# Splitting doubles on a Trainium2 core: the masked exponent and its product kept in the contiguous temporary

## The chip, the cores and the metric

One core of one Trainium2 chip runs the kernel. The metric is the device time of one execution in microseconds; before the change it is 879.73 us, the median of three runs (878.51 to 879.98). The engines are TensorE (PE, with PEld for its weight loads), VectorE (DVE), ScalarE (ACT), GpSimd (POOL) and SyncE (SP, which issues the DMAs).

## The reference

Attention with pooled queries feeds a two-layer feed-forward network, and that feeds a second network of four experts mixed by probabilities:

```python
q_pool = q.reshape(B, H, S // 2, 2, D).mean(axis=3)          # 2 x 8 heads, 1152 -> 576 queries, D = 64
scores = scale * np.matmul(q_pool, k.transpose(0, 1, 3, 2))
attn = softmax(scores); x = np.matmul(attn, v)               # -> 1152 tokens x 512
h = x @ w_in;  x = np.maximum(0.01 * h, h) @ w_out           # 512 -> 2048 -> 512
p = probs / (probs.sum(-1, keepdims=True) + 1e-09)
out = sum(p[:, e:e + 1] * (np.maximum(x @ w1[e], 0.0) @ w2[e]) for e in range(4))   # 512 -> 1024 -> 512
```

`w_in` and `w_out` reach the kernel as doubles (the set-up multiplies them by a float64 number), so each of these weights is a pair of 32-bit words in memory; the experts' weights are float32.

## The kernel before, in words

Every operand of a product is split into a higher part `h` that TensorE's float32r holds and a lower part `l`, the rest; a product is three matmuls (h by h, h by l, l by h). For the doubles this is the work of `split64` (from line 59): a tile of 128 x 512 doubles lies in SBUF as interleaved words, `L` the lower and `W` the upper word of each pair, so that both are read and written with a step of two words. `split64` returns six steps:

- s0: ACT writes the scaled upper word into a temporary `t` (L69). It is contiguous, and there are two of them in turn (tag `c` in the feed-forward stage, `kh` while the attention still runs).
- s1, s2: DVE shifts `t` (L72) and puts the sign back from `W` (L76). Without `fast`, ACT turns the lower word into a float in place (L78).
- s3: DVE masks sign and exponent of `t` into `W` (L83, called the mask below); ACT rounds `t` into `h` (L84); POOL writes `l = t - h` (L86, the subtraction).
- s4: the lower word times the masked power of two, into `L` (the product): on DVE with `fast` of 1 (L90), else on POOL (L92).
- s5: POOL adds the product to `l` (L95, the addition). With `fast` of 2, used for one weight tile only, DVE does the subtraction and the addition too.

The order of every engine's instructions is written out by hand (`manual_schedule`): each engine works through its own list, and an instruction that waits for another engine holds up all that stand behind it on its own engine. The first network's 16 tiles f of `w_in` (called a0 to a15) and of `w_out` (b0 to b15) are split as they are needed. What one f does after its first-layer matmuls is called a round here: `run(evac_leaky(f, ps), next_a(f + 2), next_b(f - 1))` interleaves the steps of the evacuation (ACT L600 and DVE L601 make `gf` out of PSUM, ACT L48 makes `gh`, DVE L55 makes `gl`) with those of two splits. `gf` has one buffer and PSUM's three-bank tiles `h` take turns between two, so a late L601 holds up TensorE's next first layer. The second layer runs in groups of tiles, one output quarter d behind each first layer: first a group of two tiles (18 matmuls a quarter, rounds 3 to 6), then groups of four, four and six (36 or 54 matmuls). L637 and L639 take those sums out of PSUM, ACT in the first group and DVE in the others. In round 15 the splits of b14 and of b15 stand one after the other ahead of the evacuation.

a0 and a1 are split during the last pair of the attention, one step for each tile of queries; a1's steps s4 and s5 stand behind the attention's last sums (`run_av(1e9)`, then `ahead` of 9 and 10). The pool of the feed-forward stage's temporaries `c` is opened in the space which the attention's pools leave, so its first tile waits for the last accesses there.

Of the kernel before, what the change touches and what calls it, by code (L numbers as in the profile page):

```python
# [13 lines left out]
U32 = mybir.dt.uint32  # L14
# [16 lines left out]
def f32(ap):  # L31
    return ap.bitcast(F32)
# [3 lines left out]
def tile_kernel(ctx: ExitStack, tc: tile.TileContext, q, k, v, w_in, w_out, probs, w1, w2, out):  # L36
# [22 lines left out]
    def split64(h, l, w, tmp, fast=0):  # L59
        """Parts of doubles, given as pairs of words: h of float32r, l with what h leaves. A list of steps, of which  # L60
        VectorE does one more with fast of 1 and all of GpSimd's with 2."""
        L, W = w[:, :, 0], w[:, :, 1]
        c = {}
        e = DVE if fast == 2 else POOL

        def s0():
            # The exponent with float32's bias: the word, read as float32, has it less 896 when scaled by 2**-112.
            c["t"] = tmp()
            ACT.mul(f32(c["t"]), f32(W), 2.0**-112)  # L69

        def s1():
            DVE.tensor_scalar(c["t"], c["t"], 3, None, op0=ALU.logical_shift_left)  # L72

        def s2():
            t = c["t"]
            DVE.scalar_tensor_tensor(t, W, -2**31, t, op0=ALU.bitwise_and, op1=ALU.bitwise_or)  # L76
            if not fast:
                ACT.mul(f32(L), L.bitcast(U32), 2.0**-52)  # L78

        def s3():  # L80
            # The lower 32 bits of the fraction, times the signed power of two.
            t = c["t"]
            DVE.tensor_scalar(W, t, -0x800000, None, op0=ALU.bitwise_and)  # L83
            ACT.copy(h, f32(t))  # L84
            # t has 21 bits and h their upper 12: l holds the difference exactly.
            e.tensor_tensor(l, f32(t), f32(h), op=ALU.subtract)  # L86

        def s4():
            if fast:
                DVE.scalar_tensor_tensor(f32(L), L.bitcast(U32), 2.0**-52, f32(W), op0=ALU.mult, op1=ALU.mult)  # L90
            else:
                POOL.tensor_tensor(f32(L), f32(L), f32(W), op=ALU.mult)  # L92

        def s5():
            e.tensor_tensor(l, f32(l), f32(L), op=ALU.add)  # L95

        return [s0, s1, s2, s3, s4, s5]

    def run(*lists):
        """The lists' steps in turn."""  # L100
        for i in range(max(map(len, lists), default=0)):
            for x in lists:
                if i < len(x) and x[i]:
                    x[i]()

# [1 line left out]
    n1 = DFF // 128  # L107
# [21 lines left out]
    def shared(i):  # L129
        """Two operands of 512 columns, where the attention has a tile of weights."""  # L130
        t = se.tile([128, S], F32R, tag=f"e{i}", name="sh", bufs=1)
        return t[:, :DM], t[:, DM:2 * DM]
# [52 lines left out]

    # Three banks of PSUM: the attention's scores; then in turn with three more.
    ps_h = [ctx.enter_context(tc.tile_pool(name="ps_h0", bufs=1, space=PSUM))]
    turn = [0]
# [18 lines left out]

    # ================= attention =================
    with ExitStack() as actx:
# [7 lines left out]
        for t in qst:  # L217
            POOL.memset(f32(t[:, :, 0, SQ:]), 0.0)
            POOL.memset(f32(t[:, :, 1, :64]), 0.0)
        # The lower parts of a pair's middle rows, each head's over its own partitions.  # L220
        qmid = [sb.tile([128, 128], F32R, tag=f"qmid{i}", name=f"qmid{i}", bufs=1) for i in range(2)]
# [6 lines left out]
        def two_heads(n, name):  # L228
            """Operands of a pair, of which every other's stay after the attention, for weights as they are loaded."""
            pool = sb if n % 2 else se  # L230
            return [pool.tile([128, S], F32R, tag=f"{name}{h}", name=name, bufs=1) for h in range(2)]
# [23 lines left out]
        def first_pair():  # L255
            """The first pair's operands; each head's rows come twice from memory, so nothing is moved between partitions."""
            b, p = pairs[0]
# [31 lines left out]
        def prep_pair(n):  # L289
            """The pair's operands, split, and the loads of the next; a list of steps."""  # L290
            # VectorE does what the first scores and products wait for.
            e_q, e_v = DVE if n == 1 else POOL, DVE if n == 0 else POOL
# [44 lines left out]

        # The q tiles of a pair: four of one head, one of 64 rows of each, four of the other.
        tiles = [(n, t) for n in range(len(pairs)) for t in range(9)]
        # The second product's share of a tile's time, in microseconds of TensorE, by the tile's place in its pair.  # L340
        AVD, AVB = 1.07, {1: 0.5}
        # How many tiles before a pair's first its operands are begun, and the tiles for the first pairs.
        P0, P1, P2 = 10, 1, 8
        # Up to this tile the scores run two tiles ahead, then three.
        L2 = 6
        # The last pair's tiles at which a feed-forward weight's split begins.
        AT0 = (0, 6)
        # Parts of the first layer that fit between the last four tiles.
        F0N = (0, 2, 2, 2)
        s_sb, chunks = {}, {}  # L350

        def emit_s(i):
            n, t = tiles[i]
            ps = three_banks(0)
            Q, K = qst[n % 2], kst[n]
            if t < 4:
                use = [(0, t * 128)]
            elif t == 4:
                use = [(0, 512), (1, 0)]
            else:  # L360
                use = [(1, 128 + (t - 5) * 128)]
            for c in range(3):
                cs = slice(c * CW, (c + 1) * CW)
                mms = [(Q[:, j, h, c0:c0 + 128], K[h][:, cs]) for h, c0 in use for j in (1, 0)]
                if len(use) > 1 and n:
                    # The rows' lower parts together, times the higher parts of both heads' keys.
                    mms = mms[::2] + [(qmid[n % 2], k_hi_of[n][:, cs])]
                for m, (x, y) in enumerate(mms):
                    PE.matmul(ps[:, c, :CW], x, y, start=m == 0, stop=m == len(mms) - 1)  # L369
            e = (sb if i % 5 > 2 else se).tile([128, S], F32, tag=f"e{i % 5}", name="e", bufs=1)  # L370
            e = e.rearrange("p (a b) -> p a b", a=3)
            st = sb.tile([128, 4], F32, tag="st", name="st", bufs=6)
            DVE.tensor_scalar(e, ps[:, :, :CW], -0.5 / float(D) ** 0.5, None,  # L373
                              op0=ALU.mult, op1=ALU.min, accum_out=st[:, 0:1])
            s_sb[i] = (e, st)
# [91 lines left out]
        with tc.manual_schedule():  # L467
            # The table of activation functions comes while the first loads run.
            DVE.memset(warm, 0.0)
            ACT.activation(warm, warm, AF.Exp)  # L470
            q_add, q_hi, q_lo, k_hi, k_lo = first_pair()
            # TensorE's clock rises while the first loads run.
            wps = ps_t.tile([128, 3, 128], F32, tag="t", name="t")
# [30 lines left out]

            # The feed-forward layers' first weights are split along with the last pair.

# [20 lines left out]

            # The operands of each pair are made ready from so many tiles before its first, the loads of the next in between.
            begin_at = {9 * m - P0: m for m in range(3, len(pairs))} | {0: 0, P1: 1, P2: 2}
            steps = {}  # L530
            for i, (n, t) in enumerate(tiles):
# [8 lines left out]
                if i == len(tiles) - 4:  # L540
                    # The last scores are done: the first layer starts with the tokens and heads that are ready.
                    f0_ps, mms = first_layer(0, xh, xl)
# [19 lines left out]

    # ================= feed-forward layers =================
    wb = ctx.enter_context(tc.tile_pool(name="wb", bufs=1))
# [13 lines left out]
    def next_b(f):  # L578
        """The f tile's second-layer weights; in the last layers those of two, at the second."""
        if f < n1:  # L580
# [10 lines left out]
    def evac_leaky(f, ps):  # L591
        """A list of steps, among which those of two calls of split64 fit."""
        s = ps[:, :, :CW]
# [80 lines left out]
    with tc.manual_schedule():  # L674
# [8 lines left out]
        run(evac_leaky(1, ps), next_b(1))  # L683
        # A second-layer tile takes the place of that eight before it, which is free when its group is done.
        when_b = {f: [f - 1] for f in range(3, 15)} | {15: [14, 15]}
        # A group's second layer runs among the next tiles' first layer.
        second = [(g, d) for g in range(len(GROUPS)) for d in range(KD)]
# [70 lines left out]
```

## Time and profile before

| | |
|---|---|
| time, median of three runs | 879.73 us (878.51 to 879.98) |
| span of the profiled execution, first to last instruction | 876.6 us |
| PE busy | 848.8 us, 97% |
| DVE, ACT, POOL busy | 472.5, 379.4, 382.6 us |
| chain that ended last | PE 75%, DVE 17%, issue 3%, ACT 2% |

The time of the profiled execution is its span of 876.6 us and what lies around it, the start and the end of the program; the page gives the span alone. A busy share is an average over stages: DVE's 40 slices read 9 in the attention and to about 350 us, then fall to 1 and 2 in the experts, so what DVE does matters in one part and not in another. In the views below a row of the timeline gives start and duration in us, the engine, the line, the operation with what it writes and reads, and in brackets the idle time before it with what ended that.

### The profile page before, as it was taken

The page shows a single profiled execution, that of the slowest core. Times are in us where ns is not written, and L with a number is a line of the kernel's source. Part 1 is how long each engine was busy: PE and PEld are TensorE (multiplying, and loading weights), DVE is VectorE, ACT ScalarE, POOL GpSimd, SP SyncE. Part 2 cuts the span into 40 slices and gives each one's busy share as a digit, 9 for nine tenths or more (in the row PEclk, how much of TensorE's full clock was granted, in tenths as well). Part 3 has the DMA queues.
Part 4 walks back from the last instruction along what each step waited for, and adds up shares of the span by engine and source line. Part 5 has one row for each costly group of instructions (what it writes and reads, how often), then busy time and mean ns, then how long its engine had stood idle before and what let it go on. Part 6 is the DMA issues. An engine that isn't in the chain of part 4 may idle for free.

```text
span 876.6 us, 12608 instructions
## 1 busy us (share of the span) xinstructions
PE 848.8 (97%) x4879; PEld 797.3 (91%) x4879; DVE 472.5 (54%) x814; ACT 379.4 (43%) x672; POOL 382.6 (44%) x330
## 2 busy tenths in 40 slices
PE   6799999999989899999999999999999999999998
PEld 5699999999989899999999998899988998889986
DVE  5989999999998999787733121112211111111211
ACT  4888998999874665334311330013200331013200
POOL 1678888898655677665510431013300332003200
PEclk7999999999999999999999999999999999999999
DMA  6446644664500233222310211001200121002011
GB/s 188 120 114 174 152 108 134 177 150 108 161 26 28 100 126 109 79 67 97 97 49 1 76 69 49 1 29 68 96 1 1 49 97 49 1 0 73 13 49 48
DMA packets 20795, 68.59 MB, mean 78 GB/s; under 512 B 2688, under 2 KB 2688, under 8 KB 20736
## 3 DMA queue, kind: packets, MB, share of 16 engines
q1 hardware_dynamic: 20736, 67.79, 26.1%
q8 instruction: 38, 0.62, 0.3%
q14 instruction: 21, 0.17, 0.1%
HBM read 48.91 MB, written 2.36 MB: 58 GB/s over the span
## 4 chain that ended last, share of the span: by engine, by line
PE 75%; DVE 17%; issue 3%; ACT 2%; POOL 1%; DMA 1%; SPq 0%; DVEq 0%; POOLq 0%; ACTq 0%
PE h L203 9%; PE h L205 9%; PE h L204 9%; PE o L664 8%; PE o L665 8%; PE o L666 8%; PE h L369 6%; PE av L438 5%; PE t L411 5%; DVE e L373 4%; DVE tl L55 3%; PE h L633 3%; PE h L632 3%; PE h L634 3%; DVE w L83 2%
## 5 line engine op out<-in xcount | busy, mean ns | idle before, releaser
L615 ACT ACTIVATE gh<-h 128x1152 fp32r<-128x1152 f32 x32 | 36.3, 1135 | 281.7 <-PE h L205 281.7
L616 DVE SCALAR_TENSOR_TENSOR gl<-h,gh 128x1152 fp32r<-128x1152 f32 x32 | 43.4, 1358 | 159.4 <-ACT gh L615 159.4
L55 POOL TENSOR_TENSOR a<-w,a 128x512 fp32r<-128x512 f32 x21 | 27.6, 1314 | 208.8 <-ACT a L48 208.8
L55 DVE TENSOR_TENSOR tl<-t,th 128x384 fp32r<-128x384 f32 (+1 forms) x240 | 112.0, 503 | 1.7 <-ACT th L415 1.6
L389 POOL TENSOR_SCALAR e<-e,st 128x1152 f32<-128x1152 f32 x70 | 86.9, 1244 | 57.4 <-DVE st L387 37.0
L369 PE MATMUL h<-k,qst 128*128 128x384 f32 x438 | 96.7, 352 | 12.6 <-DVE e L373 6.2
L373 DVE TENSOR_SCALAR_CACHE_REDUCE e<-h 128x1152 f32<-128x1152 f32 x72 | 97.4, 1353 | 16.6 <-PE h L369 15.8
L415 ACT CAST th<-t 128x384 fp32r<-128x384 f32 (+1 forms) x240 | 91.2, 458 | 24.9 <-PE t L411 24.7
L369 PEld LDWEIGHTS h<-k,qst 128*128 128x128 f32 x438 | 77.0, 195 | 17.8 <-DVE e L373 10.8
L379 ACT ACTIVATE e<-e,st 128x1152 f32<-128x1152 f32 x72 | 91.1, 1266 | 4.4 <-DVE e L373 2.0
L411 PE MATMUL t<-ident,e 128*128 128x128 f32 x648 | 84.4, 276 | 4.2 <-POOL e L389 2.6
L670 DVE SCALAR_TENSOR_TENSOR oacc<-o,pw,oacc 128x512 f32<-128x512 f32 x27 | 20.3, 751 | 125.0 <-PE o L666 125.0
L665 PE MATMUL o<-b,gh 128*128 128x512 f32 x216 | 85.2, 395 | 0.0
L664 PE MATMUL o<-b,gh 128*128 128x512 f32 x216 | 85.2, 394 | 0.0
L666 PE MATMUL o<-b,gl 128*128 128x512 f32 x216 | 85.2, 394 | 0.0
L203 PE MATMUL h<-yh,a 128*128 128x384 f32 x252 | 84.7, 336 | 0.0
L205 PE MATMUL h<-yh,a 128*128 128x384 f32 x252 | 84.7, 336 | 0.0
L204 PE MATMUL h<-yl,a 128*128 128x384 f32 x252 | 84.7, 336 | 0.0
L411 PEld LDWEIGHTS t<-ident,e 128*128 128x128 f32 x648 | 75.0, 141 | 10.1 <-POOL e L389 5.4
L55 POOL TENSOR_TENSOR sh<-w,sh 128x512 fp32r<-128x512 f32 x19 | 25.1, 1332 | 88.2 <-ACT sh L48 88.2
L438 PE MATMUL av<-tl,v 128*128 128x256 f32 (+1 forms) x288 | 51.5, 306 | 0.0
L438 PE MATMUL av<-th,v 128*128 128x256 f32 (+1 forms) x288 | 49.5, 304 | 0.0
(135 smaller groups left out, 1977.4 us busy)
## 6 DMA issues: line engine op xcount, KB each, us to landing
w<-in_w SPq DMA_DIRECT2D x32, 512.0 KB, 3.2
w<-in_w_out SPq DMA_DIRECT2D x16, 512.0 KB, 4.1
qst<-rq SPq DMA_DIRECT2D x28, 288.0 KB, 4.4
w<-in_w_in SPq DMA_DIRECT2D x14, 512.0 KB, 3.2
rv<-in_v SPq DMA_DIRECT2D x8, 576.0 KB, 5.6
rk<-in_k SPq DMA_DIRECT2D x7, 576.0 KB, 6.1
rq<-in_q SPq DMA_DIRECT2D x7, 576.0 KB, 4.7
k<-kh SPq DMA_DIRECT2D x14, 288.0 KB, 4.1
```

The source lines that it names most:

```text
L55: eng.tensor_tensor(dst, src, f32(high), op=ALU.subtract)
L203: PE.matmul(ps[:, c, :CW], wh[:, k_], src_h[:, k_, cs], start=k_ == 0, stop=False)
L204: PE.matmul(ps[:, c, :CW], wh[:, k_], src_l[:, k_, cs], start=False, stop=False)
L205: PE.matmul(ps[:, c, :CW], wl[:, k_], src_h[:, k_, cs], start=False, stop=k_ == KD - 1)
L369: PE.matmul(ps[:, c, :CW], x, y, start=m == 0, stop=m == len(mms) - 1)
L373: DVE.tensor_scalar(e, ps[:, :, :CW], -0.5 / float(D) ** 0.5, None, op0=ALU.mult, op1=ALU.min, accum_out=st[:, 0:1])
L411: PE.transpose(ps[:, j], e[:, (3 * g + j) * 128:(3 * g + j + 1) * 128], ident)
L415: ACT.copy(h, ps[:, :, s0:s0 + w])
L438: PE.matmul(cell["ps"][:, :w], V, part[:, kb, :w], start=m == 0, stop=last)
L664: PE.matmul(ps, gh[:, ts_], wh, start=m == 0, stop=False)
L665: PE.matmul(ps, gh[:, ts_], wl, start=False, stop=False)
L666: PE.matmul(ps, gl[:, ts_], wh, start=False, stop=m == EF // 128 - 1)
```

## The change

The mask goes from step s3 to step s4, and writes the temporary `t` in place instead of the upper words `W`. The product is written into `t` too instead of the lower words `L`, and the addition of s5 reads it there. The interleaved words are no longer written by these steps. Since the mask now overwrites what ACT's rounding and the subtraction read, it comes behind both; and `t` is read until s5, where its last reader was the subtraction of s3. The diff, without the comments that it also drops:

```diff
         def s3():
-            # The lower 32 bits of the fraction, times the signed power of two.
             t = c["t"]
-            DVE.tensor_scalar(W, t, -0x800000, None, op0=ALU.bitwise_and)
             ACT.copy(h, f32(t))
-            # t has 21 bits and h their upper 12: l holds the difference exactly.
+
             e.tensor_tensor(l, f32(t), f32(h), op=ALU.subtract)
 
         def s4():
+
+            t = c["t"]
+            DVE.tensor_scalar(t, t, -0x800000, None, op0=ALU.bitwise_and)
             if fast:
-                DVE.scalar_tensor_tensor(f32(L), L.bitcast(U32), 2.0**-52, f32(W), op0=ALU.mult, op1=ALU.mult)
+                DVE.scalar_tensor_tensor(f32(t), L.bitcast(U32), 2.0**-52, f32(t), op0=ALU.mult, op1=ALU.mult)
             else:
-                POOL.tensor_tensor(f32(L), f32(L), f32(W), op=ALU.mult)
+                POOL.tensor_tensor(f32(t), f32(L), f32(t), op=ALU.mult)
 
         def s5():
-            e.tensor_tensor(l, f32(l), f32(L), op=ALU.add)
+            e.tensor_tensor(l, f32(l), f32(c["t"]), op=ALU.add)
 
         return [s0, s1, s2, s3, s4, s5]
...
```

In the changed file the mask is line 89, the product 91 or 93, the addition 96, the subtraction 84 and the rounding 82. No engine gets more or fewer instructions. Names carry buffer numbers below: `tmp_3556` is the temporary of a1, `c_3718` that of a2; `c_4095` and `c_4097` those of a7 and b4, `w_3938` and `w_3940` their words, `gl` and `gf` the evacuation's parts. In brackets stand the engines whose semaphores a row waits for.

DVE where the attention ends, before: the mask of a1 stands ahead of the last two sums.

```order
L55 TENSOR_TENSOR tl_3563<-t_3614,th_3562 128x3x128 [waits Activation_49]
L83 TENSOR_SCALAR raw_2951<-tmp_3556 128x512 [waits DMAHW4_49,DMAHW3_49,DMAHW5_49,DMAHW2_49,DVE_49]
L448 TENSOR_TENSOR xf_3641<-av_3585,tmp_3640 64x320 [waits Activation_49,Pool_49]
L55 TENSOR_TENSOR xl_65<-xf_3641,xh_64 64x320 [waits Activation_49]
L448 TENSOR_TENSOR xf_3666<-av_3646,tmp_3665 64x256 [waits DVE_49,Activation_49]
L55 TENSOR_TENSOR xl_65<-xf_3666,xh_64 64x256 [waits Activation_49]
L72 TENSOR_SCALAR c_3718<-c_3718 128x512 [waits Activation_49]
L76 SCALAR_TENSOR_TENSOR c_3718<-w_3277,c_3718 128x512 [waits DMAHW0_49,DVE_49]
```

DVE at the same place after the change:

```order
L55 TENSOR_TENSOR tl_3563<-t_3614,th_3562 128x3x128 [waits Activation_49]
L449 TENSOR_TENSOR xf_3640<-av_3585,tmp_3639 64x320 [waits Activation_49,Pool_49]
L55 TENSOR_TENSOR xl_65<-xf_3640,xh_64 64x320 [waits Activation_49]
L449 TENSOR_TENSOR xf_3665<-av_3645,tmp_3664 64x256 [waits DVE_49,Activation_49]
L55 TENSOR_TENSOR xl_65<-xf_3665,xh_64 64x256 [waits Activation_49]
L89 TENSOR_SCALAR tmp_3556<-tmp_3556 128x512 [waits Pool_49]
L72 TENSOR_SCALAR c_3718<-c_3718 128x512 [waits DMAHW3_49,DMAHW4_49,DMAHW2_49,DMAHW5_49,DMAHW1_49,Activation_49]
L76 SCALAR_TENSOR_TENSOR c_3718<-w_3277,c_3718 128x512 [waits DMAHW0_49,DVE_49]
```

The mask of a1 has moved behind the last `xl` and waits for POOL; POOL's product and addition of a1, which are made of it, move with it.

DVE in the round of f = 5, from `gl` to the next round's `gf`, before:

```order
L55 TENSOR_TENSOR gl_4090<-gf_4088,gh_4089 128x1152 [waits Activation_49]
L83 TENSOR_SCALAR w_3938<-c_4095 128x512 [waits DVE_49]
L83 TENSOR_SCALAR w_3940<-c_4097 128x512 [waits DVE_49]
L90 SCALAR_TENSOR_TENSOR w_3940<-w_3940 128x512 [waits DVE_49]
L601 TENSOR_TENSOR gf_4177<-h_4140,gf_4177 128x1152 [waits Activation_49]
```

The same rows after the change:

```order
L55 TENSOR_TENSOR gl_4090<-gf_4088,gh_4089 128x1152 [waits Activation_49]
L89 TENSOR_SCALAR c_4095<-c_4095 128x512 [waits Pool_49]
L89 TENSOR_SCALAR c_4097<-c_4097 128x512 [waits Pool_49]
L91 SCALAR_TENSOR_TENSOR c_4097<-w_3940,c_4097 128x512 [waits DVE_49]
L602 TENSOR_TENSOR gf_4177<-h_4140,gf_4177 128x1152 [waits Activation_49]
```

They stand in the same order; the two masks wait for POOL where they waited for DVE alone, and the product is made in the temporary.

## Rows read from the trace of the kernel before

**Rows 1.** The page: span, and busy time of each engine (share of span, instructions).

```profile
span 876.6 us, 12608 instructions
...
PE 848.8 (97%) x4879; PEld 797.3 (91%) x4879; DVE 472.5 (54%) x814; ACT 379.4 (43%) x672; POOL 382.6 (44%) x330
```

**Rows 2.** Windows: stretch, its length, then busy us (instructions) of PE, PEld, DVE, ACT, POOL.

```profile
262.00:303.00 41.00, 36.61 (x215) 35.66 (x214) 38.03 (x44) 21.95 (x32) 21.59 (x16) 1.00 0.19 65
303.00:345.00 42.00, 41.34 (x236) 40.70 (x235) 41.46 (x38) 24.72 (x32) 33.79 (x23) 1.00 0.31 101
345.00:420.00 75.00, 75.00 (x429) 75.00 (x430) 60.30 (x60) 29.42 (x42) 45.29 (x31) 1.00 0.27 85
420.00:446.00 26.00, 25.36 (x144) 25.03 (x144) 17.28 (x18) 9.96 (x13) 13.11 (x9) 1.00 0.37 122
```

**Rows 3.** Timeline of PE where the first group's rounds end.

```profile
344.88 0.44 PE L632 MATMUL h<-gh,b 128*128 128x384 f32 x1 [0.61 <-DVE yf L639]
```

**Rows 4.** Lines of the split: duration in ns, least/median/most; first and last start.

```profile
L72 DVE TENSOR_SCALAR c<-c x30: 412/419/1568, 269.7 to 434.5; 128x512 int32<-128x512 int32 x30
...
L83 DVE TENSOR_SCALAR w<-c x30: 429/1518/1527, 270.9 to 436.4; 128x512 int32<-128x512 int32 x30
...
L83 DVE TENSOR_SCALAR raw<-tmp x2: 429/964/1498, 244.1 to 263.1; 128x512 int32<-128x512 int32 x2
...
L90 DVE SCALAR_TENSOR_TENSOR w<-w x18: 687/1410/1667, 272.1 to 436.8; 128x512 f32<-128x512 uint32 x18
...
L92 POOL TENSOR_TENSOR raw<-raw x2: 1038/1040/1042, 248.1 to 264.7; 128x512 f32<-128x512 f32 x2
```

**Rows 5.** Timeline of DVE, POOL and ACT, from round 5 into round 6.

```profile
318.38 2.29 POOL L86 TENSOR_TENSOR a<-c,a 128x512 fp32r<-128x512 f32 x1 [1.96 <-ACT a L84]
...
319.44 2.95 DVE L83 TENSOR_SCALAR w<-c 128x512 int32<-128x512 int32 x2
...
320.63 1.47 POOL L86 TENSOR_TENSOR b<-c,b 128x512 fp32r<-128x512 f32 x1
...
322.07 1.23 POOL L92 TENSOR_TENSOR w<-w 128x512 f32<-128x512 f32 x1
...
322.42 1.42 DVE L90 SCALAR_TENSOR_TENSOR w<-w 128x512 f32<-128x512 uint32 x1
...
323.00 1.26 ACT L69 ACTIVATE c<-w 128x512 f32<-128x512 f32 x2
...
323.37 1.64 POOL L95 TENSOR_TENSOR a<-a,w 128x512 fp32r<-128x512 f32 x1
...
324.97 1.30 POOL L95 TENSOR_TENSOR b<-b,w 128x512 fp32r<-128x512 f32 x1
325.03 1.87 DVE L72 TENSOR_SCALAR c<-c 128x512 int32<-128x512 int32 x2
```

**Rows 6.** Timeline of DVE and ACT where the attention ends.

```profile
268.46 0.42 DVE L55 TENSOR_TENSOR xl<-xf,xh 64x256 fp32r<-64x256 f32 x1 [0.47 <-ACT xh L48]
...
268.97 0.66 ACT L69 ACTIVATE c<-w 128x512 f32<-128x512 f32 x1 [0.54 <-DVE xl L55]
...
273.56 1.36 DVE L601 TENSOR_TENSOR gf<-h,gf 128x1152 f32<-128x1152 f32 x1
```

**Rows 7.** Timeline around round 15: splits of b13 to b15, its evacuation, TensorE's wait.

```profile
426.96 1.48 POOL L55 TENSOR_TENSOR a<-w,a 128x512 fp32r<-128x512 f32 x1
...
427.32 1.67 DVE L90 SCALAR_TENSOR_TENSOR w<-w 128x512 f32<-128x512 uint32 x1
...
432.23 1.62 POOL L86 TENSOR_TENSOR b<-c,b 128x512 fp32r<-128x512 f32 x1 [1.80 <-ACT b L84]
...
435.56 0.69 DVE L76 SCALAR_TENSOR_TENSOR c<-w,c 128x512 int32<-128x512 int32 x1
...
438.03 1.36 DVE L601 TENSOR_TENSOR gf<-h,gf 128x1152 f32<-128x1152 f32 x1 [0.51 <-ACT gf L600]
...
442.03 0.44 PE L633 MATMUL h<-gl,b 128*128 128x384 f32 x1 [0.64 <-DVE gl L55]
```

## The prediction

> **What bounds the kernel now.** I read the page first: PE is busy for 848.8 of 876.6 us [rows 1], so at most some 28 us of waiting can be won anywhere, while any delay on PE's own path is added in full. The windows say where DVE matters [rows 2]. From 262 to 345 us it works for 38.03 of 41 and 41.46 of 42 us: there it is the bound, and PE waits 4.39 and 0.66 us for it, up to the wait for L639 at 344.88 [rows 3]. From 345 to 420 us PE has no gap and DVE is idle for nearly 15 of 75 us, some 2.5 us in each of the six rounds: there a later DVE costs nothing. From 420 to 446 us PE waits 0.64 us, for the last `gl` [rows 7]. All thirty splits of the feed-forward stage lie between 269 and 437 us [rows 4].
>
> Next the split's own lines. The mask takes 429 ns at the least and 1518 at the median, L72 between 412 and 1568, L90 between 687 and 1667 [rows 4]. The round in rows 5 shows why: the masks begin at 319.44, in the middle of the subtraction L86 that ends at 320.67; the next subtraction ends at 322.10 and the second mask 0.29 us behind it, at 322.39; L92 ends at 323.30 and L90, of 0.69 us alone, at 323.84. The other way round, L95 begins at 323.37 and ends 1.17 us behind L90, where alone it takes 1.30. So DVE and POOL take turns, a whole instruction at a time, and the one that is held ends about 0.14 us sooner after its turn than its time alone. The long masks are waits for POOL, and not the price of the interleaved words.
>
> **The change part by part.** *Contiguous output.* The mask alone took 429 ns with an interleaved output, L72 412 to 419 with a contiguous one [rows 4]. The new mask is an operation of L72's shape, so between -0.02 and 0 us each; I take 0. The product on DVE is 687 ns alone; the new one lies between L72's 0.41 and that, and I take 0.69, since it still has two inputs. On POOL I take 1.04 (L92 undisturbed), with 1.30 (L95) as the other end.
>
> *Mask behind the subtraction.* Before, the mask waits for its turn while POOL subtracts, and comes between the two subtractions. Now it waits for the first one's end at 320.67 [rows 5], and the second, whose inputs have been ready, has begun by then (320.63). It ends at about 321.92 (1.30 alone), the first mask at 322.21, the second, undisturbed, at 322.56, L92's successor at 322.56 + 0.91 = 323.47 (L92 ended 0.91 behind the second mask) and L90's at 324.01 instead of 323.84: **+0.17 us**. In a round with one split the mask simply follows the subtraction, at the same price.
>
> The Trainium skill (SBUF — State Buffer, "Who interferes with whom") says that DVE and GpSimd share a port pair as an exclusive lock, which whoever issues first holds for the whole instruction. The trace agrees, by the 0.29 us above. If DVE were served first instead, the +0.17 would fall away in the six rounds with two splits, and the sum below would be 1.0 us smaller.
>
> *The temporary is free later.* L69 of the next round may overwrite `t` only when the addition has read it. Before, both L69 run from 323.00 to 324.26, beside L95 [rows 5]. Now the first waits for the first addition, at 325.18 (+0.17), the second for the second one's end, 324.97 + 1.30 + 0.17 = 326.44. It lasts some 0.67 [rows 6], so the second L72 can start at 327.18 and ends at 327.60; before, it ended at 325.03 + 1.87 = 326.90. That is 0.70 us, the 0.17 included: **+0.53 us**. ACT's queue is held too: `gh` comes behind the two L69, but ends near 328.3, and `gl` needs it only after two L76, at 328.8, so nothing more is late.
>
> *Rounds 0 to 7.* DVE is without slack here, so the delays add up: 8 x 0.17 + 4 x 0.53 (rounds 4 to 7, whose L69 follow a round that has two splits with POOL) = 1.36 + 2.12 = **3.5 us**. Lower end: the 0.53 hidden, 1.4 us. Upper end: 1.1 us in each of rounds 3 to 7 (0.4 more for waits that I have not seen: a doubled `gh` delay), 6 us.
>
> *Where the attention ends.* a1's mask now stands behind the last `xl`, which ends at 268.88 [rows 6], and POOL's product and addition of a1 behind the mask. Mask 0.43, product 1.04, addition 1.30 and three hand-overs of some 0.05 end at about 271.75. L69 of a2 writes the first `c`, in space that the attention leaves, and so waits for that addition: it starts at 271.8 instead of 268.97, **+2.8 us**. Its chain runs through to L601 at 273.56 without slack; in it the mask of a2, of 0.43, has lain beside ACT's rounding and now stands behind the subtraction: **+0.45**. TensorE also waits some 1.8 us there for a1's lower part, inside the same delay, since its later wait for L601 shrinks by as much. If L69 did not wait for the addition, L72 and L76 would still meet POOL's two instructions, +1.4; so 1.8 to 3.3 us, and I take **3.3**, since before L69 started 0.08 us behind the last `xl`, which is how a wait for the space looks.
>
> *Mask of a0, inside the attention.* It moves behind the following tile's sums and stands between them and the next scores. It may cost up to 1.1 us (1.5 held against 0.43 alone [rows 4]) or return 0.43 where it stood; PE is ahead at one place and waits at the other. I take 0.
>
> *Round 15.* b13's mask meets a16's subtraction (426.96) [rows 7], which now goes first: 428.26 + 0.29 + 0.03 + 0.69 = 429.27 for the product's end, where L90 ended at 427.32 + 1.67 = 428.99: +0.3. b14 is then split alone. Mask and product lay beside the subtraction (432.23, of 1.62) and now follow it: 432.53 + 1.30 + 0.46 + 0.72 = 435.0; b15's L72 0.43 more, and its L76 meets b14's addition, which holds until 436.35: it ends near 436.9 instead of 436.25. Then the rounding (0.7 with its hand-over), subtraction 1.35, mask 0.46 and product 0.72 stand in a row before L601: 440.0 instead of 438.03. TensorE waits for `gl` of this round already at 442.03, so this is all on the path: **+1.9**. The load of b15 may start 1.2 us earlier, once the product has read the words; nothing waits for it any more. Ends: 0.7 (if L601 of this round waited only for b15's later L76) and 2.5.
>
> *Sum.* 3.3 + 3.5 + 1.9 = **8.7 us**. After 345 us PE keeps its own pace, and 7 us of shift stay as they are. The profiled execution goes from 876.6 to 885.3 us of span; the median of the runs stands 3.1 us above the span, so the time is 879.73 + 8.7 = **888.4 us**. With all lower ends: 1.4 + 1.8 + 0.7 - 0.4 = 3.5; with all upper ends: 6 + 3.3 + 2.5 + 1.1 = 12.9.
>
> **The rivals.** *Faster: the interleaved store was the price.* If the long masks were slow because they write every other word, contiguous ones would take 0.42 us beside POOL as well. In rounds 0 to 7 that frees 14 x 1.09 us of masks and 8 x 0.72 of products, 21 us of DVE, against the 8.7 above; TensorE could then win back its waits of 4.39 + 0.66 + 0.64, and the time would be **874.0**. It decides from the point where a mask beside POOL takes less than about 1.1 us. Against it: the least of L83 is 429 ns with the same interleaved output, and L72 reaches 1568 with a contiguous one [rows 4].
>
> The Trainium skill has a rule on that side (Vector Engine (DVE) Microarchitecture Reference, "Measured stream behaviour on trn2"): a port keeps its full rate only for runs of two or more adjacent words, and an output that jumps at every element took 1.71 ns a column against 1.05. By it each interleaved write would lose an estimated 0.34 us, and the change would win about that with every mask. The trace does not agree: 429 against 412 to 419 ns.
>
> *No change.* The turns that DVE and POOL take sum to the same in either order, and DVE has room elsewhere. If the waits for POOL all fell into time that DVE spends waiting for its turn anyway, the time would be **880**. For it: POOL's subtraction is nearly always done when the mask gets its turn. Against it: the wait for `t` is longer than the time that hides it, by the 0.53 us above, and the two ends of the stage are chains without a turn to hide in.
>
> *Slower, but less.* L69 of a2 is free of the addition (1.5 less) and the four waits for `t` are hidden (2.1 less): 8.7 - 3.6 = 5.1, **884.8**. For it: POOL is idle at 268.9, and ACT has the most room of the three. Against it: ACT's list is in order, and L69 stands ahead of `gh`.
>
> *Slower by more.* L639 loses its cover of 2.5 us in the rounds where PE is the bound, or a0's mask holds up the attention by its 1.1 us. Were one round of 0.7 us longer in each of the six, and a0 at its upper end, 8.7 + 4.2 + 1.1 = 14.0: **893.7**. Against it: 0.7 is well under 2.5.
>
> **How the numbers follow.** Forecast 0.70, slower but less 0.13, slower by more 0.08, no change 0.04, faster 0.05. Differences under 0.2% (1.8 us) can't be told from none here. The three slower cases give 0.91, no change 0.04, faster 0.05. The range runs from 884.0 to 892.0: it holds the forecast, most of the smaller case and part of the larger one; what is left out is under 2 in 10.
>
> **What would show it.** Right: the mask's median stays near 1.5 us or splits into 1.5 for the first of two and 0.43 for the second; L69 of a2 begins at about 271.8, released by POOL; each of rounds 4 to 7 gets 0.7 us longer, with ACT's L69 waiting for POOL; TensorE waits about 1 us in each of these rounds, and about 2 us longer before the last group. Wrong: masks of 0.43 us throughout beside a busy POOL, rounds no longer than before, or L69 starting as early as before.

## The result, and the profile after

The changed kernel takes 890.95 us (median of four runs, 889.34 to 892.49) against 879.17 us before (879.73 until a fourth run was added): 1.0133 times as long, with a 95% interval of 1.0113 to 1.0153, so 11.8 us slower. The forecast was slower, 888.4 us, in a range of 884.0 to 892.0. The profiled execution's span grew from 876.6 to 887.4 us.

The page of the changed kernel, with the chain of waits at its end; below it the chain of the kernel before:

```profile
span 887.4 us, 12595 instructions
...
PE 851.0 (96%) x4879; PEld 798.3 (90%) x4879; DVE 456.9 (51%) x814; ACT 379.2 (43%) x672; POOL 380.0 (43%) x330
...
PE 72%; DVE 14%; POOL 6%; ACT 3%; issue 3%; DMA 1%; SPq 0%; POOLq 0%; DVEq 0%; ACTq 0%
```

```profile
PE 75%; DVE 17%; issue 3%; ACT 2%; POOL 1%; DMA 1%; SPq 0%; DVEq 0%; POOLq 0%; ACTq 0%
```

VectorE is busy for 15.6 us less than before [rows 1], and the kernel is slower; POOL has 6% of the chain, where it had 1%. The windows (columns as in [rows 2], then the granted clock of TensorE as a share of full speed, and the load of the DMA) show where the work went missing and time was lost all the same:

```profile
262.00:303.00 41.00, 34.37 (x188) 33.09 (x187) 28.32 (x40) 19.91 (x30) 18.03 (x13) 0.94 0.19 65
303.00:345.00 42.00, 40.59 (x226) 39.72 (x225) 32.60 (x35) 23.49 (x32) 29.70 (x20) 0.98 0.28 99
345.00:420.00 75.00, 73.11 (x419) 72.79 (x418) 55.71 (x61) 30.33 (x43) 44.76 (x30) 1.00 0.24 86
420.00:446.00 26.00, 26.00 (x151) 26.00 (x150) 19.02 (x21) 8.20 (x12) 14.62 (x10) 1.00 0.22 74
```

From 262 to 345 us VectorE worked for 79.5 of 83 us before [rows 2], now for 60.9. Its masks were long because they were held for their turn, and a held instruction counts as busy; now VectorE stands idle instead, waiting for a semaphore of POOL. The durations of the split's lines say the same (line, engine, operation; ns least/median/most):

```profile
L89 DVE TENSOR_SCALAR c<-c x30: 410/428/1506, 275.3 to 448.1; 128x512 int32<-128x512 int32 x30
...
L91 DVE SCALAR_TENSOR_TENSOR c<-w,c x18: 691/1680/1693, 275.8 to 448.6; 128x512 f32<-128x512 uint32 x18
...
L93 POOL TENSOR_TENSOR c<-w,c x12: 1407/1420/1433, 284.5 to 425.5; 128x512 f32<-128x512 f32 x12
L93 POOL TENSOR_TENSOR tmp<-raw,tmp x2: 1287/1294/1302, 247.9 to 269.4; 128x512 f32<-128x512 f32 x2
```

The masks fell from a median of 1518 ns to 428 [rows 4], and that returned nothing. Of two masks in a round, the first still lasts 1.50 us, held by the second subtraction, and the second 0.41. The last two lines are the surprise: POOL's product, 1040 ns undisturbed before [rows 4] and 1.23 us in a round [rows 5], takes 1294 and 1420 now.

From round 5 into round 6 (VectorE, POOL and ACT; it answers to [rows 5]):

```profile
324.89 1.35 DVE L55 TENSOR_TENSOR gl<-gf,gh 128x1152 fp32r<-128x1152 f32 x1
...
325.52 1.89 POOL L84 TENSOR_TENSOR a<-c,a 128x512 fp32r<-128x512 f32 x1 [2.92 <-ACT a L82]
...
327.37 1.28 POOL L84 TENSOR_TENSOR b<-c,b 128x512 fp32r<-128x512 f32 x1
327.44 1.83 DVE L89 TENSOR_SCALAR c<-c 128x512 int32<-128x512 int32 x2 [1.20 <-POOL a L84]
...
329.02 1.43 POOL L93 TENSOR_TENSOR c<-w,c 128x512 f32<-128x512 f32 x1 [0.36 <-DVE c L89]
329.31 1.69 DVE L91 SCALAR_TENSOR_TENSOR c<-w,c 128x512 f32<-128x512 uint32 x1
...
330.54 1.60 POOL L96 TENSOR_TENSOR a<-a,c 128x512 fp32r<-128x512 f32 x1
...
332.17 0.68 ACT L69 ACTIVATE c<-w 128x512 f32<-128x512 f32 x1 [2.96 <-POOL a L96]
...
333.42 0.67 ACT L69 ACTIVATE c<-w 128x512 f32<-128x512 f32 x1 [0.57 <-POOL b L96]
...
335.67 1.35 DVE L55 TENSOR_TENSOR gl<-gf,gh 128x1152 fp32r<-128x1152 f32 x1
```

The first mask waits for the first subtraction and lets the second go first, as forecast: the two masks last 1.83 us together, 1.5 and 0.4. Each L69 waits for an addition; before they ran beside the first one [rows 5]. The round, from one `gl` to the next, is 335.67 - 324.89 = 10.78 us long.

Where the attention ends (it answers to [rows 6]):

```profile
268.39 0.42 DVE L55 TENSOR_TENSOR xl<-xf,xh 64x256 fp32r<-64x256 f32 x1 [0.47 <-ACT xh L48]
268.85 0.43 DVE L89 TENSOR_SCALAR tmp<-tmp 128x512 int32<-128x512 int32 x1
269.36 1.30 POOL L93 TENSOR_TENSOR tmp<-raw,tmp 128x512 f32<-128x512 f32 x1 [4.66 <-DVE tmp L89]
270.74 1.26 POOL L96 TENSOR_TENSOR a<-a,tmp 128x512 fp32r<-128x512 f32 x1
...
272.03 0.66 ACT L69 ACTIVATE c<-w 128x512 f32<-128x512 f32 x1 [3.67 <-POOL a L96]
...
277.20 1.36 DVE L602 TENSOR_TENSOR gf<-h,gf 128x1152 f32<-128x1152 f32 x1
```

One chain, without a gap: mask, product, addition, and then the L69 of a2, released by the addition. It began 0.08 us behind the last `xl` before [rows 6], and begins 3.22 us behind it now.

The last splits, b14 and b15 in round 15, and TensorE's wait for them (it answers to [rows 7]):

```profile
441.47 1.29 POOL L84 TENSOR_TENSOR b<-c,b 128x512 fp32r<-128x512 f32 x1 [1.79 <-ACT b L82]
...
442.79 0.43 DVE L89 TENSOR_SCALAR c<-c 128x512 int32<-128x512 int32 x1 [2.10 <-POOL b L84]
...
446.77 1.30 POOL L84 TENSOR_TENSOR b<-c,b 128x512 fp32r<-128x512 f32 x1 [1.34 <-ACT b L82]
...
448.10 0.43 DVE L89 TENSOR_SCALAR c<-c 128x512 int32<-128x512 int32 x1 [2.12 <-POOL b L84]
...
449.17 1.35 DVE L602 TENSOR_TENSOR gf<-h,gf 128x1152 f32<-128x1152 f32 x1
...
451.76 0.44 PE L633 MATMUL h<-gh,b 128*128 128x384 f32 x1 [1.57 <-ACT gh L48]
...
453.15 0.44 PE L634 MATMUL h<-gl,b 128*128 128x384 f32 x1 [0.95 <-DVE gl L55]
```

Twice VectorE is idle for 2.1 us until a subtraction ends; TensorE waits 1.57 + 0.95 us where it waited 0.64 [rows 7].

### The profile page after: what moved, and what is told of

It is laid out like the page before. It is cut to its first block, busy times and chain, and to the rows that moved or that the text cites. A ratio compares the mean times of both kernels' runs of the same rounds, so it can differ in the third digit from the quotient of the medians.

```text
span 887.4 us, 12595 instructions
## 1 busy us (share of the span) xinstructions
PE 851.0 (96%) x4879; PEld 798.3 (90%) x4879; DVE 456.9 (51%) x814; ACT 379.2 (43%) x672; POOL 380.0 (43%) x330
## 4 chain that ended last, share of the span: by engine, by line
PE 72%; DVE 14%; POOL 6%; ACT 3%; issue 3%; DMA 1%; SPq 0%; POOLq 0%; DVEq 0%; ACTq 0%
PE h L206 9%; PE h L205 9%; PE h L204 9%; PE o L666 8%; PE o L667 8%; PE o L665 8%; PE h L370 6%; PE av L439 5%; PE t L412 5%; DVE e L374 4%; DVE tl L55 4%; PE h L634 2%; PE h L633 2%; PE h L635 2%; DVE c L89 2%
## 5 line engine op out<-in xcount | busy, mean ns | idle before, releaser
L412 PEld LDWEIGHTS t<-ident,e 128*128 128x128 f32 x648 | 74.9, 142 | 10.8 <-POOL e L390 6.1
L633 PE MATMUL h<-gh,b 128*128 128x384 f32 x144 | 48.9, 339 | 3.5 <-DVE yf L640 1.9
L204 PE MATMUL h<-xh,a 128*128 128x384 f32 x132 | 46.1, 350 | 5.8 <-DVE gf L602 5.8
```

The lines of the kernel that those rows point to most:

```text
L204: PE.matmul(ps[:, c, :CW], wh[:, k_], src_h[:, k_, cs], start=k_ == 0, stop=False)
L412: PE.transpose(ps[:, j], e[:, (3 * g + j) * 128:(3 * g + j + 1) * 128], ident)
```

## Three terms, counted in every trace

Single executions of one kernel differ by up to 4 us, and part of that lies in the attention: in the last kernel of the table its code is that of before, and its last `xl` ends at 270.69 us instead of 268.88. The traces are therefore compared from the last `xl` of the attention on, in three stretches: hand-over (end of that `xl` to the start of round 0's `gf` on VectorE: 4.68 us before), rounds (from there to round 14's `gf`: 148.34 us) and round 15 (from there to its own `gf`: 16.14 us). The table gives what each kernel has more than before, in us, and beside it the difference of the medians of its call.

| kernel | hand-over | rounds | round 15 | sum | medians |
|---|---|---|---|---|---|
| forecast | 3.3 | 3.5 | 1.9 | 8.7 | |
| the changed kernel | 3.71 | 5.33 | 2.16 | 11.2 | 11.8 |
| product alone in `t` | 0.13 | 2.53 | 0.91 | 3.6 | 2.4 |
| mask alone in `t` | 3.72 | 2.82 | 2.34 | 8.9 | 9.7 |
| contiguous output, old order | -0.01 | 0.57 | -0.04 | 0.5 | -0.2 |
| changed, a0 and a1 as before | 0.59 | 5.28 | 2.17 | 8.0 | 8.4 |
| changed, b13 to b15 as before | 3.71 | 5.28 | -0.07 | 8.9 | 7.8 |
| before, a0, a1, b13 to b15 changed | 3.13 | -0.01 | 2.16 | 5.3 | 5.9 |
| changed, TensorE kept busy | 3.70 | 5.32 | 2.17 | 11.2 | 9.9 |
| before, a3 to a5 all on VectorE | 0.01 | -1.66 | 0.00 | -1.7 | -1.0 |

The medians follow the sums to within 1.3 us.

## The experiments

**Product alone into the temporary.** The mask stays in s3 and in `W`; product and addition use `t`.

```diff
...
-                POOL.tensor_tensor(f32(L), f32(L), f32(W), op=ALU.mult)
+                POOL.tensor_tensor(f32(c["t"]), f32(L), f32(W), op=ALU.mult)
...
-            e.tensor_tensor(l, f32(l), f32(L), op=ALU.add)
+            e.tensor_tensor(l, f32(l), f32(c["t"]), op=ALU.add)
```

> The kernel before, with the product alone written into the temporary t; the mask stays in step s3 and in the interleaved words. Turns of DVE and POOL (my theory): t lives until the addition, so L69 waits for it, about +0.5 us in each of rounds 4 to 7, and a contiguous product on POOL of 1.30 us instead of 1.04 adds some 0.26 us to each of these; round 15 +0.7. Nothing is late where the attention ends (L69 of a2 stays at 269.0). In all +4.3 us, 883.5 us. If the interleaved store is the price (rival): half of its gain, DVE's products fall from 1.4 to 0.7 us, and the time is 877 us or less.

Measured: 881.80 us, 1.0035 (1.0022 to 1.0048), against 879.39: 2.4 us where 4.3 were expected, and 3.6 in the trace. This is the price of a temporary that comes free later. It lies in the rounds (2.53) and in round 15 (0.91); the hand-over has 0.13. The round from 5 to 6, by its two `gl`, first in the kernel before, then in this one:

```profile
318.17 1.34 DVE L55 TENSOR_TENSOR gl<-gf,gh 128x1152 fp32r<-128x1152 f32 x1
328.02 1.34 DVE L55 TENSOR_TENSOR gl<-gf,gh 128x1152 fp32r<-128x1152 f32 x1
```

```profile
321.11 1.35 DVE L55 TENSOR_TENSOR gl<-gf,gh 128x1152 fp32r<-128x1152 f32 x1
331.45 1.35 DVE L55 TENSOR_TENSOR gl<-gf,gh 128x1152 fp32r<-128x1152 f32 x1
```

9.85 us against 10.34: 0.49 more, where 0.53 was forecast. POOL's product is as short as before, though its output is contiguous and in another tile, so the 0.26 us a round that the expectation gave to it did not come:

```profile
L92 POOL TENSOR_TENSOR c<-w x12: 1218/1220/1229, 282.0 to 420.3; 128x512 f32<-128x512 f32 x12
L92 POOL TENSOR_TENSOR tmp<-raw x2: 1035/1038/1042, 249.4 to 266.0; 128x512 f32<-128x512 f32 x2
```

**Mask alone into the temporary.** The mask goes to s4 and into `t`; the product stays in `L`.

```diff
             t = c["t"]
-            DVE.tensor_scalar(W, t, -0x800000, None, op0=ALU.bitwise_and)
...
         def s4():
+            t = c["t"]
+            DVE.tensor_scalar(t, t, -0x800000, None, op0=ALU.bitwise_and)
...
-                POOL.tensor_tensor(f32(L), f32(L), f32(W), op=ALU.mult)
+                POOL.tensor_tensor(f32(L), f32(L), f32(t), op=ALU.mult)
```

> The kernel before, with the mask alone moved to step s4 and into t; the product stays in the interleaved words. Turns (my theory): the mask behind the subtraction costs 0.2 us a round, a1's late mask some 3.4 us where the attention ends, round 15 some 2 us, and L69 waits little, since t is free after the product: +6.9 us, 886.1 us. Together with the run of the product alone it should come to the whole change, +10 to +12. Interleaved store (rival): masks of 0.42 us beside a busy POOL, 14 of them freed by 1.1 us, 875 us.

Measured: 889.04 us, 1.0114 (1.0099 to 1.0130): 9.7 us, more than the 6.9 expected. By the sums of the table 8.9 of the 11.2 us come with the later mask; with the 3.6 of the product alone that is more than the whole, since the two overlap in round 15 (0.91 and 2.34 against 2.16). The same round is 10.28 us long, and the product is the longer one:

```profile
324.70 1.34 DVE L55 TENSOR_TENSOR gl<-gf,gh 128x1152 fp32r<-128x1152 f32 x1
334.98 1.34 DVE L55 TENSOR_TENSOR gl<-gf,gh 128x1152 fp32r<-128x1152 f32 x1
```

```profile
L93 POOL TENSOR_TENSOR w<-w,c x12: 1402/1418/1440, 285.8 to 424.3; 128x512 f32<-128x512 f32 x12
L93 POOL TENSOR_TENSOR raw<-raw,tmp x2: 1289/1292/1294, 249.1 to 270.6; 128x512 f32<-128x512 f32 x2
```

So it is where its two inputs lie that makes the product 0.25 us longer alone and 0.20 us in a round, whether the output is interleaved (here) or contiguous (the changed kernel). That they come from two tiles is not the reason. Before, the product read neighbouring words, `L` and `W` of each pair. Two of POOL's operations in the attention of the kernel before have 576 columns: one adds the two halves of one tile, 576 words apart, the other reads two tiles. They take the same time, where 1.04 us for 512 columns would make an estimated 1.17:

```profile
L309 POOL TENSOR_TENSOR rq<-rq x7: 1422/1426/1925, 26.4 to 203.4; 128x576 f32<-128x576 f32 x7
...
L55 POOL TENSOR_TENSOR v<-rv,v x14: 1417/1436/1448, 48.8 to 223.4; 128x576 fp32r<-128x576 f32 x14
```

The round gets 0.43 us longer here and 0.49 us with the product alone; the two sum to 0.92, and the changed kernel's is 0.93 longer.

**Contiguous output in the old order.** Mask and product go to the two halves of the raw tile, contiguous, with the order and the waits of before. The product is that of the mask with itself: the kernel leaves the lower words out of it.

```diff
+        words = w.rearrange("p a b -> p (a b)")
+        M, P = words[:, :DM], words[:, DM:]
...
-            DVE.tensor_scalar(W, t, -0x800000, None, op0=ALU.bitwise_and)
+            DVE.tensor_scalar(M, t, -0x800000, None, op0=ALU.bitwise_and)
...
-                POOL.tensor_tensor(f32(L), f32(L), f32(W), op=ALU.mult)
+                POOL.tensor_tensor(f32(P), f32(M), f32(M), op=ALU.mult)
...
```

> The kernel before with the same order and the same waits, but mask and product written contiguously: the mask into the first half of the weight's raw tile, the product (of the mask with itself, which leaves the lower words out, so the weights' lower parts are not the doubles') into the second half. Turns (my theory): the mask keeps a median of 1.5 us and the time is that of before, 879.2 us, at most +1.3 if POOL's product of 1.04 us becomes one of 1.30. Interleaved store (rival): masks of 0.42 and products of 0.7 us throughout, 874 us.

Measured: 879.17 us, 0.9998 (0.9988 to 1.0009). The masks:

```profile
L85 DVE TENSOR_SCALAR w<-c x30: 426/1514/1525, 271.7 to 437.8; 128x512 int32<-128x512 int32 x30
```

As long as with the interleaved output: 426 ns alone and 1514 when held, against 429 and 1518 [rows 4]. Contiguous output is worth nothing here, and the rival that expected a gain from it falls. The rule of the Trainium skill weighed in the prediction (Vector Engine (DVE) Microarchitecture Reference, "Measured stream behaviour on trn2") does not show for a step of two words: 3 ns of the estimated 0.34 us. The jumps at every element that the page lists are longer.

In this trace the granted clock fell to 0.50, the level of 1.2 GHz, from 297.4 to 300.8 us, as a wait of TensorE of 2.56 us ended; the kernel before kept 1.00 through one of 2.59 at the same place.

```profile
297.40:300.80 3.40, 3.39 (x11) 3.39 (x12) 3.40 (x6) 3.40 (x5) 1.18 (x2) 0.50 0.48 154
```

The interval between the `gl` of rounds 3 and 4 is 10.59 us here and 9.88 before. So the 0.57 us that this kernel has more in the rounds come where the clock fell; that they would be nothing without it is not shown.

**The changed kernel with a0 and a1 split as before.** The new last argument says whether a tile takes the changed form.

```diff
...
-            steps = split64(h, l, a_raw[f], tmp, fast)
+            steps = split64(h, l, a_raw[f], tmp, fast, f > 1)
...
```

> The changed kernel, with the old form of the split for a0 and a1 alone. If the end of the attention costs what I read (a1's mask and product behind the last sums, L69 of a2 behind the addition), L601 of round 0 begins at about 274.0 instead of 277.2 and the time is 890.95 - 3 = 888 us, about +8.8 on before; if that delay is hidden in TensorE's later waits, 891 us.

Measured: 887.82 us, 1.0100 (1.0085 to 1.0115). L69 of a2 is back behind the last `xl`:

```profile
268.45 0.42 DVE L55 TENSOR_TENSOR xl<-xf,xh 64x256 fp32r<-64x256 f32 x1 [0.47 <-ACT xh L48]
...
268.95 0.67 ACT L69 ACTIVATE c<-w 128x512 f32<-128x512 f32 x1 [0.54 <-DVE xl L55]
```

Of the hand-over's 3.71 us, 3.12 go with it. The 0.59 that stay are a2's own mask, now behind the subtraction. The L69 did wait for the addition.

**The changed kernel with b13 to b15 as before, and the kernel before with only a0, a1 and b13 to b15 changed.** The same argument, in the first:

```diff
...
-            return split64(h, l, b_raw[f], tmp, 1)
+            return split64(h, l, b_raw[f], tmp, 1, f < 13)
...
```

and in the second:

```diff
...
-            steps = split64(h, l, a_raw[f], tmp, fast)
+            steps = split64(h, l, a_raw[f], tmp, fast, f < 2)
...
-            return split64(h, l, b_raw[f], tmp, 1)
+            return split64(h, l, b_raw[f], tmp, 1, f > 12)
...
```

> The changed kernel, with the old form of the split for b13, b14 and b15 alone. By my theory round 15 returns its 2.1 us: 888.8 us, and TensorE's wait before the last group is 0.6 to 1.0 us again. If what the last round costs were hidden by TensorE's second layer, 891 us.

> The kernel before, with the new form for a0, a1, b13, b14 and b15 alone. By my theory 3 us where the attention ends and 2.1 us in round 15: +5.1, 884.3 us; the other splits' part of the change, about 6 to 7 us, is away. If the rounds cost nothing by themselves, 891 us.

Measured: 887.63 us, 1.0099 (1.0085 to 1.0112), and 885.69 us, 1.0076 (1.0063 to 1.0089). The first loses the round-15 term entirely (-0.07 us), the second has that term (2.16) and the hand-over without a2's mask (3.13), and its rounds are those of before (-0.01). The three terms are independent: 3.13 + 0.59 = 3.72 for the hand-over, measured 3.71.

**The changed kernel with TensorE kept busy.** In the changed kernel the granted clock falls twice to 0.50, the level of 1.2 GHz (from 287.5 to 290.9 and from 301.2 to 304.6 us), as waits of TensorE for `gf` of 2.60 and 2.06 us ended; before, it was 1.00 there [rows 2], through waits of 1.47 and 2.59 us. Ten more matmuls, whose sum nothing reads, stand ahead of the first layers of f = 3 and f = 4; the first ten end while TensorE would have waited, and it still waits 0.90 us behind them.

```diff
+            if f in (3, 4):
+                o = ps_o.tile([128, DM], F32, tag="o", name="o")
+                for _ in range(10):
+                    PE.matmul(o[:, :CW], a_t[f][0][:, 0], xh[:, 0, :CW], start=True, stop=True)
```

> The changed kernel, with ten extra matmuls ahead of the first layers of f = 3 and f = 4, into a bank of PSUM that nothing reads, while TensorE waits for L601. In the changed kernel's trace TensorE's granted clock falls to half after these two waits (287.5 to 290.9 and 301.2 to 304.6 us). If that costs 1 to 1.5 us, the time is 889.7 us and the clock stays at 1.0 there; if DVE's delay covers it, 891 us.

Measured: 889.70 us, 1.0122 (1.0107 to 1.0137), which the medians can't tell from the changed kernel: 889.70 is the time expected if the clock did cost, but the four executions (889.41 to 892.03) cover the same stretch as the changed kernel's (889.34 to 892.49). The traces can. The windows of the changed kernel, then of this one (granted clock in the third column from the right):

```profile
287.00:291.00 4.00, 3.25 (x10) 3.25 (x11) 3.37 (x4) 2.34 (x3) 2.26 (x3) 0.57 0.69 257
...
300.00:305.00 5.00, 4.06 (x14) 4.06 (x15) 4.20 (x6) 3.94 (x6) 2.06 (x2) 0.66 0.32 105
```

```profile
287.00:291.00 4.00, 3.10 (x18) 2.83 (x17) 3.36 (x4) 2.35 (x3) 2.25 (x3) 1.00 0.78 262
...
300.00:305.00 5.00, 3.96 (x23) 3.65 (x23) 4.54 (x7) 3.51 (x6) 1.88 (x2) 1.00 0.32 105
```

At full clock the rounds come to 5.32 us, at the fallen one to 5.33. The theory that the clock costs 1 to 1.5 us falls: the slow matmuls delay `gf` of round 4 by 0.86 us against this kernel (2.28 us more than round 0's shift instead of 1.42), but its `gl` by nothing (2.18 and 2.20): VectorE and POOL bound these rounds, and the delay is gone by their next step.

**The kernel before with a3 to a5 all on VectorE.** If POOL and VectorE only hold each other up in the first rounds, the steps may as well run on VectorE.

```diff
-        run(evac_leaky(0, f0_ps), next_a(3), next_b(0))
+        run(evac_leaky(0, f0_ps), next_a(3, 2), next_b(0))
-                run(evac_leaky(f, ps), next_a(f + 2, f == 2), *[next_b(b) for b in when_b.get(f, [])])
+                run(evac_leaky(f, ps), next_a(f + 2, 2 if f < 4 else 0), *[next_b(b) for b in when_b.get(f, [])])
```

> The kernel before, with the subtractions, products and additions of a3 to a5 on DVE (fast of 2) in rounds 0 to 3, so that POOL holds up fewer of DVE's instructions there. If taking turns with POOL is what bounds these rounds, TensorE's waits before f = 4 shrink by 1 to 2 us and the time is 876.7 us; if DVE's own work bounds them, 880 us or above.

Measured: 878.76 us, 0.9987 (0.9978 to 0.9996) against 879.79: 1.0 us faster, less than the 0.2% that can be told with certainty. Neither of the two expected times came, 876.7 us or 880 and above; the rounds in its trace are 1.66 us shorter. The attention ends 1.81 us later in this trace, so the windows begin at the end of its last `xl`, of the kernel before and then of this one:

```profile
268.88:303.00 34.12, 29.73 (x169) 28.78 (x168) 32.73 (x37) 19.35 (x25) 17.59 (x12) 1.00 0.23 78
```

```profile
270.69:304.81 34.12, 30.32 (x174) 29.68 (x173) 32.64 (x44) 19.24 (x24) 8.68 (x6) 1.00 0.24 78
```

POOL works 8.9 us less, VectorE has 44 instructions instead of 37 and no more busy time: what it took over cost it what it had waited.

## Why the prediction was right, and where it fell short

*Contiguous output: 0, right for VectorE.* The old order with contiguous output gives 0.9998. The clause on POOL was the wrong choice between two ends: 1.04 us was taken for L92's successor, and 1.30 came, the price of POOL's other instructions of this size. The rows had it: L92 alone read neighbouring words, and L95, whose inputs lie apart, took 1.30 [rows 5].

*Mask behind the subtraction, +0.17 a round, and the temporary free later, +0.53.* The mechanism is the one forecast, row by row. The second was 0.49 by the product alone in `t`. The first can be read behind the `gl` of round 5: the second mask ended 322.39 - 318.17 = 4.22 us after it before, and 329.27 - 324.89 = 4.38 now, so the order costs 0.16. POOL's product ended 5.13 us after that `gl` before and 5.56 now, 0.43 more, so 0.27 of them are the longer product; the mask alone in `t` lengthened the round by the same 0.43. Together 0.93 instead of 0.70 in a round: the step that failed is the price of POOL's product, which the sum had at nothing. The signs named for the masks came in their second form, 1.50 and 0.41. TensorE's wait of about 1 us in each of rounds 4 to 7 came once, 1.12 us long, ending at 332.32 us; in the trace with the clock kept up there are two, of 1.09 and 1.08, so the slow matmuls had left TensorE behind.

*Rounds, 3.5 us.* They came to 5.33, within the upper end of 6 but with the wrong size. In the changed trace four intervals between `gl` (3 to 7) grew by 0.91 each instead of 0.70, by the longer product; the interval from round 2 to 3 grew by 0.73 where 0.17 was counted, because the wait for `t` begins a round earlier than forecast; and the others grew by 0.96 together. Of these, 0.38 lie between the `gl` of rounds 8 and 9, behind 345 us, where the sum let the shift stay as it was: TensorE waits 1.89 us there for L640, where it waited 0.61 for L639 [rows 3]. This is the term that was mis-sized most.

*Where the attention ends, 3.3 us.* 3.71: the L69 of a2 began 3.13 us later instead of 2.8, of which 0.26 is the product again, and a2's mask cost 0.59 instead of 0.45. The mask of a0, taken at 0, shows no price: the last `xl` of the attention ended at 268.81 us, before at 268.88. Two traces of the same attention differ there by 1.81 us, so a smaller price is not excluded.

*Round 15, 1.9 us.* 2.16, with TensorE waiting 1.9 us longer, as forecast.

*The sum* is 11.2 us instead of 8.7 counted from the attention's end. The span grew by 10.8, since the program ended 0.3 us sooner behind the issue of the output's last transfer, and the attention ended 0.07 sooner. The other executions of the changed kernel are up to 3.2 us longer than the profiled one; what lies in them is not shown. Two of the four, 892.24 and 892.49, lie above the range, and the median 1.05 us inside its end: the mechanism was right, but the forecast of 888.4 was 2.5 us short.

*The rivals.* Faster: fell, by contiguous masks as long as before. No change: fell; VectorE did get room, 18.6 us of it before 345 us, but as idle time ahead of POOL. Slower but less: fell, both for a2's L69 and for the waits for `t`. Slower by more: its price of 893.7 was almost as near to the result as the forecast, but its mechanism did not come in the six rounds. `gf` of round 8 starts 8.25 us later than before, and that of rounds 9 to 14 8.97, in every one of them: apart from the wait ahead of round 9, L639's cover held.

## What to carry to other kernels

Here an instruction that waited for its turn was made to wait for a semaphore: its engine's busy time fell by 18.6 us in the bound stage, and the chain got longer. Such an edit is judged by the distance between two evacuations, and not by the engine's busy time. A temporary that is kept in use longer costs what the next writer has to wait, and that may be read from the trace ahead of the change. Before the inputs of an operation are moved apart, look for an instruction of that engine whose inputs lie apart already, and take its duration.

## What was not expected of the hardware

- POOL's product of 128x512 took 1.04 us when its inputs were the two words of each pair, or one operand read twice, and 1.29 us when the second input lay elsewhere; where the output went made no difference (1.04 into another tile, 1.29 into the same). One tile for both inputs is not enough: halves of one tile, 576 words apart, cost as much as two tiles (1.43 us for 576 columns). How near the words must lie is not shown.
- TensorE's clock fell to 1.2 GHz at the end of waits of 2.60 and 2.06 us in the changed kernel, and that cost this kernel's end nothing, because VectorE and POOL bound those rounds. The kernel before waited 2.59 us at full clock.
